# Merging the state weightings of an S4 channel loop on VectorE, and moving a state copy to ScalarE

## The chip, the cores and the metric

The kernel runs on one core of a Trainium2 chip. A core has five engines that run their own instruction streams: TensorE (PE in the profile, its weight loads PEld), VectorE (DVE), ScalarE (ACT), GpSimd (POOL) and SyncE (SP, which issues DMAs here). They wait for each other by semaphores. The metric is the device time of one execution in microseconds, lower is better. The kernel before has a median of 2704.61 us in three runs (2699.75 to 2706.55).

## The reference, cut to what matters

The program computes a gated mix of an attention block and of a state space convolution (S4), and all gradients of it. The part in question is the S4 branch:

```
P = exp(logdA[:, :, None] * l)                 # D channels, N = 128 states, L = 2048 steps
K = einsum("dn,dnl,dn->dl", C, P, dt * B).real # a convolution kernel for each channel
y = irfft(rfft(u) * rfft(K)) + u * Dskip       # causal convolution, D = 576
out = g * attention(x) + (1 - g) * y           # g: a sigmoid gate for each token
```

The kernel computes the convolution and its gradients without a Fourier transform. The 2048 steps are cut into 16 blocks of 128. Inside a block of steps matmuls do the work; from block to block each state is multiplied by z^128 (a complex number per channel and state) and the next block's contribution is added. That is a scan over 15 steps for each channel, run once for the forward direction (called h) and once for the gradient (called g). The scanned states are weighted by w = C * dt * B * z, complex again, and go into matmuls that give y and the gradient of u.

## The kernel before, in words

The program has four stages. The first (up to about 120 us) projects x, prepares the per-channel parameters and stores them in a DRAM tensor `par_d`. The second is attention, forward and backward, to about 2090 us. Beside it GpSimd builds a basis `E_d` for the channel loop. The third, from about 2090 to 2532 us, is the channel loop. The last computes the parameter gradients and the output projections.

The channel loop (L1479) goes over 18 blocks of 32 channels, `i` being the block; states lie on the 128 partitions. Its order on TensorE, ScalarE, VectorE and GpSimd is written out by hand: instructions stand in each engine's queue as the loop emits them. An iteration works on several blocks: it weights and uses the scanned states of block `i`, it scans the second half of block `i` together with the first half of block `i + 1`, and it prepares the input states of block `i + 2` (`sb`) and the loads of block `i + 3` (`mb`).

What the change and the steps of the prediction touch, in the order of an iteration:

- `scan_open` (L707 to L711) makes the tile `HG` of a block's scanned states (real and imaginary part, 15 steps, two directions, 32 channels, float32, two buffers) and copies the first step's states from `UV`, on VectorE. It is called for block `i + 1` at the start of iteration `i`.
- `scan` (L713 to L735) has three VectorE instructions for each step of a chain: a product with the parameter rows 0 to 3 into `tz` (L730), the new input added (L733), and the sum of both parts into `HG` (L735), which reads the second part with its real and imaginary halves reversed. Two chains run alternately, 7 steps each, 42 instructions for an iteration.
- `rw1` (L745 to L750) weights the finished states of block `i` with two real parameter rows. It makes `wa` = `HG` times row 4 and `wb` = `HG` times row 5, 1920 elements each on every partition.
- `rw2` (L752 to L756) makes `Rw`, the complex product in bfloat16, from the halves of `wa` and `wb`: the real half by a subtraction, the imaginary half by -1 and a subtraction, 960 elements each.
- `turn_e` (L658, TensorE transposes and ScalarE copies of the basis into `E1e`), `t0` (L779), `ybp` (L788, matmuls of `Rw` into `yp`), `uv` (L691, matmuls `uvp` and ScalarE evacuations into `UV`, L705).
- `cast1` (L737) casts the states of each direction to bfloat16 (`hR`, `gR`) on ScalarE.
- `pairs1` and `pairs2` (L822 to L840) have VectorE multiply states with states into two tiles `pq`, which lie in the same memory as `wa` and `wb` (tags `wA` and `wB`, one buffer each), and TensorE sums them into `misc`.
- `sums` (L848) has GpSimd add up results of block `i - 1` in two small instructions (L851, L852); `m_part` (L614) and `prep_rx` (L592) feed later blocks, with ScalarE evacuations `mst` and `RX`.
- `load_par` (L673) brings two blocks' parameter rows 0 to 7 from `par_d` into one of two buffers, on GpSimd's DMA queue. Rows 6 and 7 hold weights for another product (`wk_cast`, L758), rows 8 and 9 are read outside the loop.

In the first stage `pars` (L316) fills `par_d` in eleven steps; the last one (L360 to L363) writes rows 4 and 5. In the last stage VectorE, ScalarE and GpSimd are ordered by a scheduler; two row tiles `rowb` and `rowb2` hold outputs 10 and 11 before their stores (L1729 to L1732), and both are used again near the end (L1796).

Of the kernel before, what the change touches and what calls it, by code (L numbers as in the profile page):

```python
# [17 lines left out]
P = 128  # L18


def build(tc, aps, dbg_aps=None, stages=("s1", "attn", "post", "s4", "final")):
# [40 lines left out]
    with ExitStack() as gctx:  # L62
# [27 lines left out]
        NS = NB - 1  # L90
        SUB = 16
        NSUB = P // SUB
        NPAR = 10
        INV2PI = float(1.0 / (2.0 * np.pi))
        MW = P + SUB
        EQ = 4
# [32 lines left out]
        with ExitStack() as ctx:  # L129
# [186 lines left out]
            def pars(k):  # L316
                prm, dt_b, ath, tp, Wn, wz = [prm_t[n_] for n_ in ("prm", "dt", "ath", "tp", "W", "wz")]
                gm, c_, s_, q_ = [zt[:, y] for y in range(4)]
                bc = dt_b.unsqueeze(1).to_broadcast([P, 2, D])
                if k == 0:  # L320
                    AC.activation(dt_b, prm_t["tmpb"], ACT.Exp)
                    tt(ath, prm[:, 0:2, :], bc, A.mult)
                elif k == 1:
                    for y, p_ in enumerate((1, P)):
                        AC.activation(gm[:, y, :], ath[:, 0, :], ACT.Exp, scale=float(p_))
                        V.tensor_scalar(s_[:, y, :], ath[:, 1, :], float(p_) * INV2PI, None, op0=A.mult)
                    V.tensor_scalar(c_, s_, MAGIC, -MAGIC, op0=A.add, op1=A.add)
                elif k == 2:
                    tt(s_, s_, c_, A.subtract)
                    AC.activation(c_, s_, ACT.Sin, scale=0.5 * TWO_PI)  # L330
                elif k == 3:
                    AC.activation(q_, s_, ACT.Sin, scale=0.25 * TWO_PI)
                elif k == 4:
                    tt(Wn[:, 2:4, :], prm[:, 4:6, :], prm[:, 2:4, :], A.mult)
                    tt(tp, prm[:, 4:6, :], prm[:, 3:1:-1, :], A.mult)
                    tt(Wn[:, 0, :], Wn[:, 2, :], Wn[:, 3, :], A.subtract)
                elif k == 5:
                    tt(Wn[:, 1, :], tp[:, 0, :], tp[:, 1, :], A.add)
                    tt(Wn[:, 0:2, :], Wn[:, 0:2, :], bc, A.mult)
                    V.tensor_scalar(Wn[:, 2:4, :], Wn[:, 0:2, :], -1.0, None, op0=A.mult)  # L340
                    GP.dma_start(par_d[:, 6:8, :], Wn[:, 2:4, :])
                    GP.dma_start(dt_d, dt_b)
                    GP.dma_start(prm_d, prm)
                elif k == 6:
                    tt(q_, q_, q_, A.mult)
                    V.scalar_tensor_tensor(s_, q_, -0.5, c_, op0=A.add, op1=A.mult)
                elif k == 7:
                    V.scalar_tensor_tensor(s_, s_, -4.0, gm, op0=A.mult, op1=A.mult)
                    tt(c_, c_, c_, A.mult)
                elif k == 8:  # L350
                    V.scalar_tensor_tensor(c_, c_, -0.5, gm, op0=A.add, op1=A.mult)
                    V.tensor_scalar(c_, c_, -2.0, None, op0=A.mult)
                    V.tensor_scalar(q_[:, 1, :], s_[:, 1, :], -1.0, None, op0=A.mult)
                    GP.dma_start(par_d[:, 8:10, :], zt[:, 1:3, 0, :])
                    GP.dma_start(par_d[:, 1:4, :], zt[:, 1:4, 1, :])
                    GP.dma_start(par_d[:, 0:1, :], zt[:, 1:2, 1, :])
                elif k == 9:
                    tt(wz, Wn[:, 0:2, :], zt[:, 1:3, 0, :], A.mult)
                    tt(tp, Wn[:, 0:2, :], zt[:, 2:0:-1, 0, :], A.mult)
                else:  # L360
                    tt(wz[:, 0, :], wz[:, 0, :], wz[:, 1, :], A.subtract)
                    tt(wz[:, 1, :], tp[:, 0, :], tp[:, 1, :], A.add)
                    GP.dma_start(par_d[:, 4:6, :], wz)  # L363

            steps = [(m, which, pr) for m in (0, 4, 1, 2, 3) for which in (1, 0, 2) for pr in range(2)]
            stgs, sqs = {}, {}
# [121 lines left out]
        def basis_ops(pool, k0, k1):  # L488
# [18 lines left out]

            def load_z(k):
                ez[k] = pool.tile([P, 2, CE], F32, tag="ez", bufs=2, name="ez")
                nc.gpsimd.dma_start(ez[k], par_d[:, 8:10, k * CE:(k + 1) * CE])  # L510

            def emit_power(dst, src, lo, n, sq):

# [157 lines left out]
        pars_ = {}  # L671

        def load_par(b, dma=nc.gpsimd.dma_start):  # L673
            par = pars_[b] = Q["pl"].tile([P, 8, XB], F32, tag="par", bufs=2, name="par")
            dma(par, par_d[:, 0:8, b * XB:(b + 1) * XB])

        def par_of(b):
            return pars_[b // 2][:, :, b % 2 * CB:(b % 2 + 1) * CB]
# [28 lines left out]
        def scan_open(b):  # L707
            B_ = blk(b)
            HG = B_["HG"] = Q["pw"].tile([P, 2, NS, 2, CB], F32, tag="HG", bufs=2, name="HG")
            UVk = B_["UVk"] = B_["UV"][:, :, 0:2 * NB, :].rearrange("p r (s k) c -> p r s k c", s=2)  # L710
            nc.vector.tensor_copy(HG[:, :, 0], UVk[:, :, :, 0, :])  # L711

        def scan(*chains):  # L713

# [29 lines left out]

        def rw1(b):  # L745
            B_ = blk(b)
            for nm, r_, tg in (("wa", 4, "wA"), ("wb", 5, "wB")):
                B_[nm] = Q["pw"].tile([P, 4 * NS, CB], F32, tag=tg, name=nm)
                nc.vector.tensor_tensor(B_[nm], B_["HG"].rearrange("p r k s c -> p (r k s) c"),  # L749
                                        par_of(b)[:, r_, :].unsqueeze(1).to_broadcast([P, 4 * NS, CB]), op=A.mult)  # L750

        def rw2(b):  # L752
            B_ = blk(b)
            wa, wb, Rw = B_.pop("wa"), B_.pop("wb"), B_["Rw"]
            nc.vector.tensor_tensor(Rw[:, 0], wb[:, 2 * NS:], wa[:, 0:2 * NS], op=A.subtract)
            nc.vector.scalar_tensor_tensor(Rw[:, 1], wa[:, 2 * NS:], -1.0, wb[:, 0:2 * NS], op0=A.mult, op1=A.subtract)  # L756

        def wk_cast(b):  # L758
            wk = blk(b)["wk"] = Q["pw"].tile([P, 2, CB], BF, tag="wk", bufs=2, name="wk")
            nc.scalar.copy(wk, par_of(b)[:, 6:8, :])  # L760

        def k0(b):

# [58 lines left out]
        def pairs1(b):  # L822
            B_ = blk(b)
            UV, hR, gR = B_["UV"], B_["hR"], B_["gR"]
            B_["pq"] = pq = [Q["pw"].tile([P, 2, 2, 2, NS, CB], BF, tag=tg, name="pq") for tg in ("wA", "wB")]
            pmul(pq[0][:, 0], UV[:, :, CV0:CV0 + NS, :], hR)
            psum(b, 0, [pq[0][:, 0]], NS)

# [581 lines left out]
        if "s4" in stages:  # L1410
# [8 lines left out]
            with ExitStack() as ctx:  # L1419
# [27 lines left out]
                with tc.manual_schedule(engines={mybir.EngineType.SP}):  # L1447
# [114 lines left out]
        if "final" in stages and "s4" in stages:  # L1562
# [7 lines left out]
            with ExitStack() as ctx:  # L1570
# [33 lines left out]
                with ExitStack() as actx:  # L1604
# [22 lines left out]
                    rowb = tile_("rowb", [P, D], BF, "dlrowb")[0:1]  # L1627
                    rowb2 = tile_("rowb2", [P, D], BF, "ddsrowb")[0:1]
# [3 lines left out]
                    nc.sync.dma_start(zB, par_d[:, 8:10, :])  # L1632
# [7 lines left out]
                    nc.sync.dma_start(Wri, par_d[:, 6:8, :])  # L1640
# [84 lines left out]
                    for u, (f0, fsz) in enumerate(HALF):  # L1725
                        rp = pps.tile([P, 512], F32, tag="one", name="fr")
                        mm(rp[0:1, 0:fsz], lhsT=ones_f[:, 0:1], rhs=Tb[:, f0:f0 + fsz])
                        nc.vector.tensor_tensor(row[:, f0:f0 + fsz], rp[0:1, 0:fsz], dt_b[0:1, f0:f0 + fsz], op=A.mult)
                    nc.vector.tensor_copy(rowb, row)  # L1729
                    nc.gpsimd.dma_start(aps_out["out_10"].rearrange("(o d) -> o d", o=1), rowb)  # L1730
                    nc.vector.tensor_copy(rowb2, dDs_row)
                    nc.gpsimd.dma_start(aps_out["out_11"].rearrange("(o d) -> o d", o=1), rowb2)  # L1732

                ctx.enter_context(tc.manual_schedule(engines={mybir.EngineType.PE}))
                for t in range(NT):
# [57 lines left out]
                    nc.vector.tensor_copy(dgwb[HP * j:HP * j + 1, :], pgw[HP * j:HP * j + 1, 0:DQ])  # L1793
                    nc.sync.dma_start(aps_out["out_12"][j * DQ:(j + 1) * DQ].rearrange("(o d) -> o d", o=1), dgwb[HP * j:HP * j + 1, :])
                for c, (f0, fsz) in enumerate(dch[0:nf]):
                    ob = tile_(("row", "rowb", "rowb2")[c % 3], [P, D], BF, "dwo_bf")  # L1796
# [17 lines left out]
                ob = tile_(("row", "rowb", "rowb2")[c % 3], [P, D], BF, "dwo_bf")  # L1814
# [52 lines left out]
```

## Time and profile before

| what | value |
| --- | --- |
| runs, median (lowest to highest) | 2704.61 us (2699.75 to 2706.55) |
| the profiled execution, its own time | 2687.22 us |
| its span | 2685.5 us, mean granted TensorE clock 0.972 |
| busy: TensorE, VectorE, ScalarE, GpSimd | 2404.0 (90%), 2299.9 (86%), 2345.2 (87%), 1787.2 (67%) us |
| chain that ended last, by engine | ACT 40%, PE 25%, DVE 24% |
| 0 to 167 us (first stage and start of attention) | PE busy 140.45, DVE 90.83, ACT 94.41 |
| 167 to 2050 us (attention) | PE busy 1689.53, DVE 1684.16, ACT 1858.98 |
| 2142 to 2350 us (channel loop) | PE busy 200.24, DVE 199.27, ACT 186.72, POOL 87.93 |
| 2350 to 2530 us (channel loop) | PE busy 169.84, DVE 177.03, ACT 137.76, POOL 79.72 |
| 2530 to 2685.5 us (last stage) | PE busy 145.45, DVE 98.05, ACT 27.07 |
| `wa` and `wb`, 18 each | median 2359 and 2351 ns (2159 and 2151 at least) |
| `Rw`, its two halves | median 1158 and 1151 ns |
| `HG` copy (L711), 18 | median 227 ns |

The profiled execution is one run of its own, shorter than the three timed ones. Every duration below is from it. A row of the order of time gives the start in us, the busy time of the row's instructions in us, the engine, the line, the operation, what it writes and reads with partitions x elements, how many instructions are merged, and in brackets how long the engine was idle before it and what ended that. A row of a stretch of time gives, after the stretch and its length, busy time and count for PE, PEld, DVE, ACT and POOL, then the granted clock, the busy share of the DMA engines and their GB/s. An engine's instructions are issued a little before the one ahead of them has ended, so neighbouring rows overlap by up to 0.2 us.

### The profile page before, as it was taken

How to read it: one execution, taken by the hardware profiler on the slowest of the kernel's cores; microseconds unless marked ns; L12 is line 12 of the kernel's file. 1: busy time of each engine (PE TensorE's matmuls, PEld its weight loads, DVE VectorE, ACT ScalarE, POOL GpSimd, SP SyncE). 2: the span in 40 equal slices, each digit the busy share in tenths (PEclk: the TensorE clock that was granted, in tenths of full speed). 3: DMA queues.
4: the chain of work that ended last, by engine and by line, in shares of the span. 5: the costliest groups of instructions: out<-in, count | busy, mean ns of one | idle time of the engine just before them, and what ended most of it. 6: DMA issues, size and time to landing. Idle time of an engine off the chain costs nothing.

```text
span 2685.5 us, 70035 instructions
## 1 busy us (share of the span) xinstructions
PE 2404.0 (90%) x27411; PEld 1141.2 (42%) x27411; DVE 2299.9 (86%) x4142; ACT 2345.2 (87%) x2727; POOL 1787.2 (67%) x2827
## 2 busy tenths in 40 slices
PE   8798898998988899988999989989887699999999
PEld 4433333333333333333333333333332598998656
DVE  4749999999998999989999988999997599999964
ACT  5489999999999999999999999999995498989221
POOL 0178888888888788888888888887831144444331
PEclk8989999999999999999999999999997699999999
DMA  7637889879979978997898898789669788988995
GB/s 230 189 96 157 155 162 180 165 152 184 172 153 168 181 161 159 177 175 152 167 177 152 161 171 163 155 163 180 149 138 199 182 243 251 254 253 247 268 260 129
DMA packets 1156229, 485.45 MB, mean 181 GB/s; under 512 B 1070517, under 2 KB 1110054, under 8 KB 1153594
## 3 DMA queue, kind: packets, MB, share of 16 engines
q1 hardware_dynamic: 1110138, 341.36, 64.2%
q0 software_dynamic: 43744, 134.11, 18.5%
q10 hardware_dynamic: 2016, 5.51, 0.6%
q8 instruction: 214, 3.51, 0.6%
q14 instruction: 117, 0.96, 0.1%
HBM read 145.68 MB, written 93.21 MB: 89 GB/s over the span
## 4 chain that ended last, share of the span: by engine, by line
ACT 40%; PE 25%; DVE 24%; issue 6%; DMA 3%; SPq 1%; ACTq 0%; POOL 0%; DVEq 0%; POOLq 0%
ACT eb L1384 24%; ACT PT L1379 15%; DVE ds L1389 8%; PE ps_P L30 7%; DVE tz L730 3%; PE accV L30 2%; PE ps_dx L30 2%; PE turn_p L1092 2%; DVE tz L733 2%; DVE HG L735 1%; DVE pq L810 1%; DVE wa L749 1%; PE accK L30 1%; DVE wb L749 1%; DVE dvacc L1146 1%
## 5 line engine op out<-in xcount | busy, mean ns | idle before, releaser
L1389 DVE TENSOR_TENSOR ds<-ps_P,PT 128x512 bf16<-128x512 f32 x2048 | 1312.2, 683 | 120.8 <-PE ps_P L30 83.2
L1384 ACT ACTIVATE eb<-ps_P 128x1024 bf16<-128x1024 f32 x1024 | 1101.4, 1076 | 30.3 <-PE ps_P L30 30.3
L1379 ACT ACTIVATE PT<-ps_P 128x1024 bf16<-128x1024 f32 x1024 | 1106.8, 1081 | 19.4 <-PE ps_P L30 18.0
L30 PE MATMUL ps_P<-dOaT,VaT_g 32*128 32x512 bf16 x2048 | 580.4, 386 | 32.2 <-DVE ds L1389 16.6
L503 POOL TENSOR_TENSOR et<-eG,eT 128x448 f32<-128x448 f32 x576 | 542.2, 961 | 10.7
L30 PE MATMUL ps_P<-QaT_g,KaT_g 32*128 32x512 bf16 x2048 | 401.7, 385 | 138.0 <-ACT PT L1379 124.4
L30 PE MATMUL ps_P<-KaT_g,QaT_g 32*128 32x512 bf16 x2048 | 404.1, 387 | 1.2 <-ACT eb L1384 0.6
L30 PEld LDWEIGHTS <-KaT_g 32*128 32x128 bf16 x2048 | 147.9, 91 | 467.6 <-issue 452.0
L503 POOL TENSOR_TENSOR Eo<-et,et 128x448 bf16<-128x448 f32 x288 | 326.9, 1135 | 20.7
L30 PEld LDWEIGHTS <-QaT_g 32*128 32x128 bf16 x2048 | 116.1, 91 | 283.0 <-issue 260.4
L30 PE MATMUL accV<-eb,dOa 128*32 128x512 bf16 x2048 | 184.9, 394 | 27.4 <-ACT eb L1384 27.3
L30 PE MATMUL accO<-PT,Vtok_g 128*32 128x512 bf16 x2048 | 206.5, 392 | 0.1
L30 PE MATMUL accK<-dsT,Qtok_g 128*32 128x256 bf16 x4096 | 161.5, 278 | 14.1 <-DMA dsT<-ds 12.4
L30 PE MATMUL accQ<-ds,Ktok_g 128*32 128x512 bf16 x2048 | 159.9, 390 | 2.3 <-DVE dvacc L1146 2.2
L30 PEld LDWEIGHTS <-Vtok_g 128*32 128x32 bf16 x2048 | 52.7, 93 | 222.7 <-issue 222.7
L1097 DVE COPY dsT<-turn_p 128x1024 bf16<-128x1024 bf16 (+1 forms) x216 | 139.2, 644 | 2.7 <-PE turn_p L1092 2.7
L1092 PE MATMUL turn_p<-ident_bf,ds 128*128 128x128 bf16 x1664 | 133.7, 223 | 1.9 <-DVE gb L1164 1.0
L669 ACT COPY E1e<-etp 128x1024 bf16<-128x1024 bf16 x132 | 125.1, 1052 | 4.6 <-PE etp L668 4.4
L503 POOL TENSOR_TENSOR et<-eT 128x32 f32<-128x32 f32 (+3 forms) x288 | 115.9, 422 | 11.4
L30 PEld LDWEIGHTS <-Qtok_g 128*32 128x32 bf16 x4096 | 87.5, 96 | 78.6 <-issue 64.9
L1092 PEld LDWEIGHTS <-ds 128*128 128x128 bf16 x1664 | 96.9, 99 | 49.3 <-issue 49.3
L1044 POOL TENSOR_TENSOR dOa<-dO_b,rl 128x288 bf16<-128x288 bf16 x32 | 21.5, 672 | 143.7 <-DVE rl L1039 143.6
(292 smaller groups left out, 3742.0 us busy)
## 6 DMA issues: line engine op xcount, KB each, us to landing
E_d<-Eo POOLq DMA_DIRECT2D x144, 256.0 KB, 3.5
E1n<-E_d POOLq DMA_DIRECT2D x30, 1024.0 KB, 7.4
T0w<-Kp_d SPq DMA_DIRECT2D x18, 1024.0 KB
xs<-xb_d POOLq DMA_DIRECT2D x28, 512.0 KB, 9.9
dsT<-ds SPq DMA_TRANSPOSE x512
dqkv_d<-dtk POOLq DMA_DIRECT2D x96, 72.0 KB, 4.2
Md_d<-mst SPq DMA_DIRECT2D x18, 288.0 KB
skw<-Md_d SPq DMA_DIRECT2D x72, 64.0 KB
```

The source lines that it names most:

```text
L30: return nc.tensor.matmul(out, lhsT=lhsT, rhs=rhs, start=start, stop=stop, **kw)
L503: nc.gpsimd.tensor_tensor(out, a, b, op=op)
L669: copy(E_[:, 4 * q:4 * q + 4], pt_)
L730: nc.vector.tensor_tensor(tz[x], HG[:, :, k - 1].unsqueeze(1).to_broadcast([P, 2, 2, n, CB]), ZZ.unsqueeze(3).to_broadcast([P, 2, 2, n, CB ...
L733: nc.vector.tensor_tensor(tz[x][:, 0], tz[x][:, 0], UVk[:, :, :, k, :], op=A.add)
L735: nc.vector.tensor_tensor(HG[:, :, k], tz[x][:, 0], tz[x][:, 1, ::-1], op=A.add)
L749: nc.vector.tensor_tensor(B_[nm], B_["HG"].rearrange("p r k s c -> p (r k s) c"), par_of(b)[:, r_, :].unsqueeze(1).to_broadcast([P, 4 * NS ...
L1092: nc.tensor.transpose(pt_[:, x, qb, :], t_[:, qb * P:(qb + 1) * P], ident_bf)
L1097: (nc.scalar.copy if NTOT <= now[0] < NTOT + OFF else nc.vector.tensor_copy)(o_(), pt_[:, x:x + n])
L1379: nc.scalar.activation(U["PT"][i, j // 2], ps, ACT.Exp)
L1384: nc.scalar.activation(e, ps, ACT.Exp)
L1389: nc.vector.tensor_tensor(U["ds"][i][:, j, :], ps, U["PT"][i, j // 2][:, j % 2, :], op=A.mult)
```

## The change

The parameter rows get the signs: `par_d` has 12 rows, rows 4 to 7 are -wr, -wr, -wi, wi, and what stood in rows 6 to 9 stands in rows 8 to 11. With these, one VectorE instruction makes both weightings in a tile `wab` (3840 elements on every partition, `HG` read twice, the row of each part read by a broadcast), and one more adds part 0 and the reversed part 1 into both halves of `Rw` (1920 elements). The copy of the first states goes to ScalarE for all blocks but the first, and stands directly behind the evacuation of the states it reads, one iteration earlier than before. The products `pq` and `wab` share one memory of the size of the two before. To make room for the two more parameter rows, the row of output 11 shares `rowb` with that of output 10, output 11 being stored first.

```diff
@@ pars, last step
-                    GP.dma_start(par_d[:, 4:6, :], wz)
+                    V.tensor_scalar(tp, wz, -1.0, None, op0=A.mult)
+                    GP.dma_start(par_d[:, 4:5, :], tp[:, 0:1, :])
+                    GP.dma_start(par_d[:, 5:7, :], tp)
+                    GP.dma_start(par_d[:, 7:8, :], wz[:, 1:2, :])
@@ load_par
-            par = pars_[b] = Q["pl"].tile([P, 8, XB], F32, tag="par", bufs=2, name="par")
-            dma(par, par_d[:, 0:8, b * XB:(b + 1) * XB])
+            par = pars_[b] = Q["pl"].tile([P, 10, XB], F32, tag="par", bufs=2, name="par")
+            dma(par, par_d[:, 0:10, b * XB:(b + 1) * XB])
@@ scan_open
-            nc.vector.tensor_copy(HG[:, :, 0], UVk[:, :, :, 0, :])
+            (nc.vector.tensor_copy if b == 0 else nc.scalar.copy)(HG[:, :, 0], UVk[:, :, :, 0, :])
@@ rw1
-            for nm, r_, tg in (("wa", 4, "wA"), ("wb", 5, "wB")):
-                B_[nm] = Q["pw"].tile([P, 4 * NS, CB], F32, tag=tg, name=nm)
-                nc.vector.tensor_tensor(B_[nm], B_["HG"].rearrange("p r k s c -> p (r k s) c"),
-                                        par_of(b)[:, r_, :].unsqueeze(1).to_broadcast([P, 4 * NS, CB]), op=A.mult)
+            wab = B_["wab"] = Q["pw"].tile([P, 2, 2, 2 * NS, CB], F32, tag="wA", name="wab")
+            h_ = B_["HG"].rearrange("p r k s c -> p r (k s) c").unsqueeze(1).to_broadcast([P, 2, 2, 2 * NS, CB])
+            w_ = par_of(b)[:, 4:8].rearrange("p (m r) c -> p m r c", r=2).unsqueeze(3).to_broadcast([P, 2, 2, 2 * NS, CB])
+            nc.vector.tensor_tensor(wab, h_, w_, op=A.mult)
@@ rw2
-            wa, wb, Rw = B_.pop("wa"), B_.pop("wb"), B_["Rw"]
-            nc.vector.tensor_tensor(Rw[:, 0], wb[:, 2 * NS:], wa[:, 0:2 * NS], op=A.subtract)
-            nc.vector.scalar_tensor_tensor(Rw[:, 1], wa[:, 2 * NS:], -1.0, wb[:, 0:2 * NS], op0=A.mult, op1=A.subtract)
+            wab, Rw = B_.pop("wab"), B_["Rw"]
+            nc.vector.tensor_tensor(Rw, wab[:, 0], wab[:, 1, ::-1], op=A.add)
@@ pairs1
-            B_["pq"] = pq = [Q["pw"].tile([P, 2, 2, 2, NS, CB], BF, tag=tg, name="pq") for tg in ("wA", "wB")]
+            pq = Q["pw"].tile([P, 4, 2, 2, NS, CB], BF, tag="wA", name="pq")
+            B_["pq"] = pq = [pq[:, 0:2], pq[:, 2:4]]
@@ channel loop
                     uv(1, 1)
+                    scan_open(1)
...
                         if nx:
-                            scan_open(i + 1)
                             scan((i, KH, NS, None), (i + 1, 1, KH, None))
...
                         if sb is not None:
                             uv(sb, 1)
+                            scan_open(sb)
@@ last stage
-                    nc.vector.tensor_copy(rowb, row)
-                    nc.gpsimd.dma_start(aps_out["out_10"].rearrange("(o d) -> o d", o=1), rowb)
                     nc.vector.tensor_copy(rowb2, dDs_row)
                     nc.gpsimd.dma_start(aps_out["out_11"].rearrange("(o d) -> o d", o=1), rowb2)
+                    rowb = tile_("rowb", [P, D], BF, "dlrowb")[0:1]
+                    nc.vector.tensor_copy(rowb, row)
+                    nc.gpsimd.dma_start(aps_out["out_10"].rearrange("(o d) -> o d", o=1), rowb)
```

The remaining lines of the diff move the rows 6 to 9 to 8 to 11 where they are written and read, and let the last stage's output tile take the memory of `Tb` where it took that of `rowb2`.

More of the change, by code (lines that the diff above doesn't have):

```diff
@@ L92, in build @@
         NSUB = P // SUB
-        NPAR = 10
+        NPAR = 12
         INV2PI = float(1.0 / (2.0 * np.pi))
@@ L340, in pars @@
                     V.tensor_scalar(Wn[:, 2:4, :], Wn[:, 0:2, :], -1.0, None, op0=A.mult)
-                    GP.dma_start(par_d[:, 6:8, :], Wn[:, 2:4, :])
+                    GP.dma_start(par_d[:, 8:10, :], Wn[:, 2:4, :])
                     GP.dma_start(dt_d, dt_b)
@@ L353, in pars @@
                     V.tensor_scalar(q_[:, 1, :], s_[:, 1, :], -1.0, None, op0=A.mult)
-                    GP.dma_start(par_d[:, 8:10, :], zt[:, 1:3, 0, :])
+                    GP.dma_start(par_d[:, 10:12, :], zt[:, 1:3, 0, :])
                     GP.dma_start(par_d[:, 1:4, :], zt[:, 1:4, 1, :])
@@ L509, in load_z @@
                 ez[k] = pool.tile([P, 2, CE], F32, tag="ez", bufs=2, name="ez")
-                nc.gpsimd.dma_start(ez[k], par_d[:, 8:10, k * CE:(k + 1) * CE])
+                nc.gpsimd.dma_start(ez[k], par_d[:, 10:12, k * CE:(k + 1) * CE])
             def emit_power(dst, src, lo, n, sq):
@@ L746, in rw1 @@
             B_ = blk(b)
-            for nm, r_, tg in (("wa", 4, "wA"), ("wb", 5, "wB")):
-                B_[nm] = Q["pw"].tile([P, 4 * NS, CB], F32, tag=tg, name=nm)
-                nc.vector.tensor_tensor(B_[nm], B_["HG"].rearrange("p r k s c -> p (r k s) c"),
-                                        par_of(b)[:, r_, :].unsqueeze(1).to_broadcast([P, 4 * NS, CB]), op=A.mult)
+            wab = B_["wab"] = Q["pw"].tile([P, 2, 2, 2 * NS, CB], F32, tag="wA", name="wab")
+            h_ = B_["HG"].rearrange("p r k s c -> p r (k s) c").unsqueeze(1).to_broadcast([P, 2, 2, 2 * NS, CB])
+            w_ = par_of(b)[:, 4:8].rearrange("p (m r) c -> p m r c", r=2).unsqueeze(3).to_broadcast([P, 2, 2, 2 * NS, CB])
+            nc.vector.tensor_tensor(wab, h_, w_, op=A.mult)
         def rw2(b):
             B_ = blk(b)
-            wa, wb, Rw = B_.pop("wa"), B_.pop("wb"), B_["Rw"]
-            nc.vector.tensor_tensor(Rw[:, 0], wb[:, 2 * NS:], wa[:, 0:2 * NS], op=A.subtract)
-            nc.vector.scalar_tensor_tensor(Rw[:, 1], wa[:, 2 * NS:], -1.0, wb[:, 0:2 * NS], op0=A.mult, op1=A.subtract)
+            wab, Rw = B_.pop("wab"), B_["Rw"]
+            nc.vector.tensor_tensor(Rw, wab[:, 0], wab[:, 1, ::-1], op=A.add)
         def wk_cast(b):
             wk = blk(b)["wk"] = Q["pw"].tile([P, 2, CB], BF, tag="wk", bufs=2, name="wk")
-            nc.scalar.copy(wk, par_of(b)[:, 6:8, :])
+            nc.scalar.copy(wk, par_of(b)[:, 8:10, :])
         def k0(b):
@@ L1626, in build @@
                     row = tile_("row", [P, D], F32, "dlrow")[0:1]
-                    rowb = tile_("rowb", [P, D], BF, "dlrowb")[0:1]
-                    rowb2 = tile_("rowb2", [P, D], BF, "ddsrowb")[0:1]
+                    rowb2 = tile_("rowb", [P, D], BF, "ddsrowb")[0:1]
                     pfw = Q["pbw"] = ctx.enter_context(tc.tile_pool(name="pfw", reuse_waits="tile", bufs=2))
                     nc.sync.dma_start(zA, par_d[:, 0:4:2, :])
-                    nc.sync.dma_start(zB, par_d[:, 8:10, :])
+                    nc.sync.dma_start(zB, par_d[:, 10:12, :])
                     nc.sync.dma_start(wo_sb[:, 0:nf, :], wo[0:nf * P, :].rearrange("(c p) n -> p c n", p=P))
@@ L1639, in build @@
                     nc.sync.dma_start(O_tok[:, :, 0:D], O_d)
-                    nc.sync.dma_start(Wri, par_d[:, 6:8, :])
+                    nc.sync.dma_start(Wri, par_d[:, 8:10, :])
                     Wr_n, Wi_n = Wri[:, 0, :], Wri[:, 1, :]
@@ L1728, in build @@
                         nc.vector.tensor_tensor(row[:, f0:f0 + fsz], rp[0:1, 0:fsz], dt_b[0:1, f0:f0 + fsz], op=A.mult)
+                    nc.vector.tensor_copy(rowb2, dDs_row)
+                    nc.gpsimd.dma_start(aps_out["out_11"].rearrange("(o d) -> o d", o=1), rowb2)
+                    rowb = tile_("rowb", [P, D], BF, "dlrowb")[0:1]
                     nc.vector.tensor_copy(rowb, row)
                     nc.gpsimd.dma_start(aps_out["out_10"].rearrange("(o d) -> o d", o=1), rowb)
-                    nc.vector.tensor_copy(rowb2, dDs_row)
-                    nc.gpsimd.dma_start(aps_out["out_11"].rearrange("(o d) -> o d", o=1), rowb2)
                 ctx.enter_context(tc.manual_schedule(engines={mybir.EngineType.PE}))
@@ L1795, in build @@
                 for c, (f0, fsz) in enumerate(dch[0:nf]):
-                    ob = tile_(("row", "rowb", "rowb2")[c % 3], [P, D], BF, "dwo_bf")
+                    ob = tile_(("row", "rowb", "Tb")[c % 3], [P, D], BF, "dwo_bf")
                     for u, (e0, esz) in enumerate(HALF):
@@ L1813, in build @@
                            start=(t == 0), stop=(t == NT - 1), tile_position=(0, u * HB))
-                ob = tile_(("row", "rowb", "rowb2")[c % 3], [P, D], BF, "dwo_bf")
+                ob = tile_(("row", "rowb", "Tb")[c % 3], [P, D], BF, "dwo_bf")
                 nc.scalar.copy(ob[0:HB, 0:DH2], ps[0:HB, 0:DH2])
```

## The prediction

> **What bounds the kernel now.** I read the page's top for the share of each engine, then the busy time by stage, then the waits and the order of time of the stage that the change touches.
>
> ```profile
> core 0: us, PE busy (x) PEld busy (x) DVE busy (x) ACT busy (x) POOL busy (x), PEclk, DMA share, GB/s
> 167.00:2050.00 1883.00, 1689.53 (x18160) 589.08 (x18159) 1684.16 (x2780) 1858.98 (x2016) 1527.01 (x2495) 0.99 0.85 163
> 2142.00:2350.00 208.00, 200.24 (x3687) 188.27 (x3680) 199.27 (x472) 186.72 (x292) 87.93 (x84) 0.98 0.85 246
> ```
>
> Attention (167 to 2050 us) is ScalarE's, 99% busy, and the change leaves its order alone. The channel loop (2142 to 2530) is 18 blocks, 13 of which take 21.84 us each from one `wa` to the next; VectorE, TensorE and ScalarE all stand over 90% there. So the question is which link closes the loop from block to block. VectorE in one block, then the TensorE and ScalarE rows that lie beside it:
>
> ```profile
> 2345.98 2.35 DVE L749 TENSOR_TENSOR wa<-HG,par 128x1920 f32<-128x1920 f32 x1
> 2348.25 2.35 DVE L749 TENSOR_TENSOR wb<-HG,par 128x1920 f32<-128x1920 f32 x1
> 2350.64 1.16 DVE L755 TENSOR_TENSOR Rw<-wb,wa 128x960 bf16<-128x960 f32 x1
> 2351.72 1.15 DVE L756 SCALAR_TENSOR_TENSOR Rw<-wa,wb 128x960 bf16<-128x960 f32 x1
> 2352.97 2.23 DVE L810 TENSOR_TENSOR pq<-UV,hR 128x1920 bf16<-128x1920 bf16 x2
> 2355.12 1.15 DVE L810 TENSOR_TENSOR pq<-UV,gR 128x1920 bf16<-128x1920 bf16 x1
> 2356.19 1.16 DVE L838 TENSOR_TENSOR pq<-gR,hR 128x896 bf16<-128x896 bf16 x2
> 2357.33 0.23 DVE L711 CAST HG<-UV 128x128 f32<-128x128 bf16 x1
> 2357.47 0.75 DVE L730 TENSOR_TENSOR tz<-HG,par 128x256 f32<-128x256 f32 x2
> ```
>
> ```profile
> 2351.85 0.21 PE L30 MATMUL yp<-Rw,E1n 128*128 128x30 bf16 x1
> 2352.92 1.82 PE L30 MATMUL yp<-Rw,E1n 128*128 128x30 bf16 x31 [0.86 <-DVE Rw L756]
> 2354.57 1.97 PE L30 MATMUL uvp<-RX,E1e 128*128 128x64 bf16 x32
> ```
>
> ```profile
> 2355.23 2.07 ACT L705 ACTIVATE UV<-uvp 128x512 bf16<-128x512 f32 x4 [0.51 <-PE uvp L30]
> 2357.16 2.02 ACT L599 COPY RX<-RXn 128x1024 bf16<-128x1024 bf16 x1
> ```
>
> `Rw` ends at 2351.72 + 1.15 = 2352.87, 6.89 us after `wa` began. From there two chains run to the next scan. One is TensorE, then ScalarE: `yp`, `uvp`, `UV` ends at 2357.30, which is 4.43 after `Rw`. The other is VectorE's own five products, over at 2357.35. The first-state copy L711 starts at 2357.33, 0.03 after `UV` and about 0.06 after VectorE could have taken it. So VectorE never shows a wait here, and yet both chains arrive together: work taken off VectorE between `Rw` and the scan is worth only what the other chain also loses. Only the stretch from `wa` to `Rw`'s end is on both.
>
> TensorE waited 0.86 us for `Rw` (its row), so it is not the bound until a block is about 0.9 us shorter. In the stretches 2256.5 to 2280.4 and 2389.7 to 2412.7, of 23.9 and 23.0 us, the granted clock is 0.93 instead of 1.00: there TensorE is late.
>
> **The weightings.** Today one block has two 1920-element products and two 960-element sums. Without disturbance (the last block):
>
> ```profile
> 2518.60 2.16 DVE L749 TENSOR_TENSOR wa<-HG,par 128x1920 f32<-128x1920 f32 x1
> 2520.68 2.15 DVE L749 TENSOR_TENSOR wb<-HG,par 128x1920 f32<-128x1920 f32 x1
> 2522.86 1.16 DVE L755 TENSOR_TENSOR Rw<-wb,wa 128x960 bf16<-128x960 f32 x1
> 2523.94 1.15 DVE L756 SCALAR_TENSOR_TENSOR Rw<-wa,wb 128x960 bf16<-128x960 f32 x1
> ```
>
> Durations are 2.00 + 0.16 for 1920 elements and 1.00 + 0.16 for 960: one element per 0.96 GHz cycle and a fixed part. But starts are closer: `wa` to `wb` 2.08, `Rw` to `Rw` 1.08 (fixed part 0.08, since neither needs the other), and `wb` to `Rw` 2.18 (0.18, since it does). All four: 2525.09 - 2518.60 = 6.49. After: 3840 elements, then the dependent sum of 1920: 4.00 + 0.18 + 2.00 + 0.16 = 6.34. Merging drops just the two cheap boundaries, 0.15 per block. The element count is the same, and nothing suggests that the broadcast or reversed patterns are slower: `wa` reads its parameters by a broadcast, and L735 a reversed half, at one element per cycle (293 ns for 128).
>
> [...] Summed as durations, two instructions less are 0.31 per block and the copy 0.23, together 0.54, over 17 blocks 9.2 us. The starts say that about half of a fixed part lies under the neighbour, and I take them: 0.15.
>
> In the middle blocks `wa` and `wb` each take 0.20 more (2.35). GpSimd's two small sums lie beside them:
>
> ```profile
> 2344.61 1.71 POOL L851 TENSOR_TENSOR SS<-m 128x96 f32<-128x96 f32 x1
> 2346.28 2.31 POOL L852 TENSOR_TENSOR SS<-m 128x96 f32<-128x96 f32 x1
> ```
>
> All of the first sum's executions (minimum, median and maximum in ns):
>
> ```profile
> L851 POOL TENSOR_TENSOR SS<-m x17: 404/1762/5967, 2167.7 to 2514.5; 128x96 f32<-128x96 f32 x17
> ```
>
> Undisturbed they take 0.40 (minimum 404 ns). In this block the first ends 0.34 after `wa` starts, the second 0.34 after `wb` starts: each gets in at an instruction's start and delays it 0.20. [...] I keep two delays of 0.20, one at the product, one at the sum: 6.74 against 6.89, still 0.15. If one slips into the products (0.06 to 0.1 of slack) a block gains at most 0.1 more; at 0.40 each it loses 0.40.
>
> TensorE's first `yp` matmul now waits for the whole `Rw`, so 32 instead of 31 follow: 1.82 / 31 = 0.06 later.
>
> **The first states on ScalarE.** VectorE loses 0.23 of work, 0.14 by starts. ScalarE's new copy stands directly behind the last `UV` and needs it. Nearest row: ScalarE's `CK` copy L1510, 128 elements, 0.29 to 0.35. With 0.03 ahead and 0.04 to VectorE: the second `tz` (the only one that waits for it) starts 0.36 after `UV`'s end. Today it starts at about 2357.80, 0.50 after. Gain 0.14 on that chain; bounds for the copy are 0.23 (L776, 32 elements) and 0.47 (L650), so 0.20 to -0.05. Behind the copy stand `RX`, `yd` and the `misc` evacuations, 0.2 later; they end in ScalarE's wait of 1.40 us for `psM` before `mst`, which hides it. Without that cover it would be 0.2 per block.
>
> Per block: second `tz` at 6.74 + 4.43 + 0.06 + 0.36 = 11.59 after the product's start, then 10.02 of scan as now (2357.80 to 2367.82): 21.61 against 21.84, 0.23 less. VectorE's own chain would allow 6.74 + 0.10 + 4.30 + 0.33 + 10.02 = 21.49, so ScalarE's copy closes the loop, not VectorE.
>
> **What costs nothing.** One tile for the products: the merged product now waits for the last reads of all four product tiles; TensorE has ended them some 6.3 us earlier, in the middle of the scan (without this cover, whatever of 6.3 is lost). Parameter loads of 10 instead of 8 rows come over a block ahead; GpSimd waited 2.31 us for `wb` to issue them and will wait about as long. Stage 1 gains a negation, 1152 elements (0.76, L340), and two more GpSimd DMA issues (0.56, L363): VectorE idles 0.66 and 1.56 us soon after, and GpSimd 14 us. In the last stage the row for output 10 waits for the store of output 11, which was issued at 2533.6 and landed 7.5 us later, against 2578.3. All zero; at most 0.8 together.
>
> **Sum.** 13 blocks at 0.23: 3.0. Blocks 0, 5 and 11, where TensorE is late, get the copy's 0.14 each: 0.4. Blocks 16 and 17, with no next state, 0.15 each: 0.3. Together 3.7 us: 2687.2 to 2683.5 in the profiled execution. That one lies 17.4 under the median of the runs, 2704.6, so 2700.9 there.
>
> **Rivals.** [...] 0.18. (b) TensorE's throttle: one more stretch at 0.93 costs 1 to 2 us, as the two do now (23.9 and 23.0 against 21.84), and leaves 2703; less waiting makes TensorE denser. 0.14. (c) Slower: ScalarE's copy is the late link. Nothing lies behind `UV` but it; if the second `tz` came over 0.50 + 0.15 = 0.65 after `UV` the block would lose. At 1.0 (copy at 0.47, waits of 0.25 on either side) that is 0.35 x 15 = 5 us, 2710; 0.3% takes 1.2. Against: L1510's 0.29, and ScalarE's 0.51 of idle just before. 0.10. That the change does not do what it says is excluded by the order of the built program: VectorE has 52 instructions less, ScalarE 17 more.
>
> **The numbers.** The forecast (2 to 6 us less) has 0.58. About 0.3%, 8.1 us, is what a measurement can tell from no change. Faster by more: most of (a), 0.17. Slower by more: the far part of (c) and what I did not see, 0.08. Within: 0.75. The range runs from (a) with a margin, 2694, to (b) with the runs' own spread of some 4 us, 2707.
>
> **What would show it.** `wab` about 4.36 and `Rw` about 2.36 beside GpSimd's sums (4.16 and 2.16 in the last block); `wab` to `Rw`'s end 6.74; block period 21.6; the second `tz` released by ScalarE's `HG`; TensorE's wait for `Rw` down to about 0.6. A period of 21.3 or less, or `wab` above 4.6, would prove me wrong.

## The result, and the profile after

The changed kernel takes 2688.6 us (median of 20 runs, 2678.8 to 2702.3). The kernel before, run beside it and counted with its first three runs, has 2695.2 us in 20 runs (2691.3 to 2706.6; 2694.7 in the 17 without those three). The ratio is 0.9973, with a 95% interval of 0.9962 to 0.9985: 6.6 us less, where 3.7 less was predicted. The predicted 2700.9 lies 12.3 us too high, and the range of 2694 to 2707 does not hold the time. Two steps went wrong, and the larger is not about the change at all. "That one lies 17.4 under the median of the runs, 2704.6, so 2700.9 there" took the median of three runs for the kernel's level, and it lies 9.4 us above the median of 20. The smaller is that the change brought more than the sum allowed.

The profiled execution took 2685.73 us, its span is 2683.9 (before: 2687.22 and 2685.5). The stretch of the loop that was shown of before (its length; busy time and count of PE, PEld, DVE, ACT and POOL; the granted clock; DMA share; GB/s):

```profile
2142.00:2350.00 208.00, 196.64 (x3684) 185.69 (x3685) 199.11 (x459) 188.90 (x300) 104.33 (x84) 0.99 0.87 251
```

VectorE has 13 instructions fewer in it and is as busy as before (199.27): the engines' shares do not show the gain, only the length of the blocks does. Next the order of time of VectorE in one block of the channel loop, the one that answers to the block shown of before (start in us, busy us, engine, line, operation, shapes, instructions merged):

```profile
2346.23 4.34 DVE L753 TENSOR_TENSOR wab<-HG,par 128x3840 f32<-128x3840 f32 x1
2350.61 2.23 DVE L758 TENSOR_TENSOR Rw<-wab 128x1920 bf16<-128x1920 f32 x1
2352.94 2.23 DVE L812 TENSOR_TENSOR pq<-UV,hR 128x1920 bf16<-128x1920 bf16 x2
2355.09 1.15 DVE L812 TENSOR_TENSOR pq<-UV,gR 128x1920 bf16<-128x1920 bf16 x1
2356.16 1.16 DVE L841 TENSOR_TENSOR pq<-gR,hR 128x896 bf16<-128x896 bf16 x2
2357.22 0.87 DVE L733 TENSOR_TENSOR tz<-HG,par 128x256 f32<-128x256 f32 x2
```

`Rw` ends at 2350.61 + 2.23 = 2352.84, 6.61 us after the product began (6.89 before, 6.74 predicted). The five pair products follow as they did. The two `tz` are new in kind: together they span 0.87 instead of 0.75, because the second waits. For what, ScalarE's order of time in the same block shows:

```profile
2355.24 2.06 ACT L708 ACTIVATE UV<-uvp 128x512 bf16<-128x512 f32 x4 [0.43 <-PE uvp L30]
2357.34 0.30 ACT L714 CAST HG<-UV 128x128 f32<-128x128 bf16 x1
```

`UV` ends at 2357.30, the copy runs from 2357.34 to 2357.64, and the second `tz` starts 0.36 after the end of `UV`, as predicted (0.50 before). The block lasts 21.47 us. Ten of the blocks 1 to 15 last 21.46 to 21.52, where before most lasted 21.84 and the prediction had 21.61. TensorE in the same block:

```profile
2352.89 1.87 PE L30 MATMUL yp<-Rw,E1n 128*128 128x30 bf16 x32 [0.87 <-DVE Rw L758]
```

All 32 `yp` matmuls now stand behind the whole `Rw` (31 before). The wait for `Rw` was 0.34 to 0.93 in most blocks, about 0.7 in the middle. And the two groups of the merged instructions over all 18 blocks (minimum, median and maximum in ns):

```profile
L753 DVE TENSOR_TENSOR wab<-HG,par x18: 4153/4345/4359, 2145.8 to 2516.0; 128x3840 f32<-128x3840 f32 x18
L758 DVE TENSOR_TENSOR Rw<-wab x18: 2157/2230/2237, 2150.0 to 2520.2; 128x1920 bf16<-128x1920 f32 x18
```

The minima are blocks without GpSimd's sums beside them. GpSimd's second sum in the same form:

```profile
L855 POOL TENSOR_TENSOR SS<-m x17: 392/4296/4306, 2173.2 to 2513.7; 128x96 f32<-128x96 f32 x17
```

It now waits out the whole product and takes 4.30 us (2.31 before). Beside the sums the product is 0.19 longer, as predicted, but the merged sum only 0.07 and not 0.20. That is the first sign of where the additional gain comes from.

Over the loop, from the first product's start to the last one's, 370.24 us against 376.41: 6.2 less. Of this the undisturbed blocks explain about 5.4: 13 blocks by 0.36, blocks 0, 5 and 11 by the copy's 0.14 (the prediction's figure, which a block that TensorE holds up cannot show) and block 16 by 0.27. Block 17's 0.15 lies behind the last product's start and brings the sum to 5.5. The rest lies in the blocks where TensorE is late, which are not the same ones from run to run (the last experiment).

### The profile page after: what moved, and what is told of

Its sections match the earlier page's. It is cut to its first block, busy times and chain, and to the rows that moved or that the text cites. A ratio compares the mean times of both kernels' runs of the same rounds, so it can differ in the third digit from the quotient of the medians.

```text
span 2683.9 us, 69949 instructions
## 1 busy us (share of the span) xinstructions
PE 2404.7 (90%) x27411; PEld 1137.9 (42%) x27411; DVE 2293.8 (85%) x4090; ACT 2350.8 (88%) x2744; POOL 1818.0 (68%) x2829
## 4 chain that ended last, share of the span: by engine, by line
ACT 40%; PE 28%; DVE 18%; issue 6%; DMA 4%; POOL 2%; SPq 1%; ACTq 0%; DVEq 0%; POOLq 0%
ACT eb L1387 23%; ACT PT L1382 14%; DVE ds L1392 7%; PE ps_P L30 7%; PE accV L30 2%; PE ps_dx L30 2%; PE turn_p L1095 2%; PE ps_dwq L30 2%; DVE tz L733 2%; PE ps_proj L30 2%; DVE wab L753 2%; PE yp L30 2%; PE accK L30 1%; DVE dvacc L1149 1%; DVE tz L736 1%
## 5 line engine op out<-in xcount | busy, mean ns | idle before, releaser
L30 PE MATMUL accK<-dsT,Qtok_g 128*32 128x256 bf16 x4096 | 162.3, 279 | 14.5 <-DMA dsT<-ds 12.4
L1047 POOL TENSOR_TENSOR dOa<-dO_b,rl 128x288 bf16<-128x288 bf16 x32 | 21.5, 673 | 149.9 <-DVE rl L1042 149.9
```

The source lines that it names most:

```text
L30: return nc.tensor.matmul(out, lhsT=lhsT, rhs=rhs, start=start, stop=stop, **kw)
```

## The experiments

The periods of the blocks separate the theories, not the times of single executions: those of one kernel spread over more than 20 us (2678.8 to 2702.3 above), while an undisturbed block's period repeats within 0.06 us. Where no number of runs is given, a kernel ran once (2681 to 2699 us, the late copy apart).

**Each half of the change alone.** First the merging without the move; the copy stays on VectorE, ahead of the scan:

```
-            (nc.vector.tensor_copy if b == 0 else nc.scalar.copy)(HG[:, :, 0], UVk[:, :, :, 0, :])
+            nc.vector.tensor_copy(HG[:, :, 0], UVk[:, :, :, 0, :])
...
                         if nx:
+                            scan_open(i + 1)
...
                             uv(sb, 1)
-                            scan_open(sb)
```

> The merged weightings alone, the first-state copy on VectorE at its old place. Theory (the loop closes from the sum's end over yp, uvp, UV and then the copy): the sum ends 6.61 us after the product's start, UV at 11.08, the copy starts 0.03 later, the second tz at 11.59, and a block takes 21.61. That is 0.13 more than with the copy on ScalarE (21.48) and 0.23 less than before (21.84). Rival (the merging was worth the 0.15 that I predicted, and the copy's move the rest): 21.69.

Measured: `Rw` ends at 6.61, `UV` at 11.08, period 21.61 to 21.65 in the undisturbed blocks. VectorE's order of time at the end of a block of this kernel whose product started at 2349.11:

```profile
2359.05 1.15 DVE L841 TENSOR_TENSOR pq<-gR,hR 128x896 bf16<-128x896 bf16 x2
2360.24 0.23 DVE L714 CAST HG<-UV 128x128 f32<-128x128 bf16 x1
2360.39 0.75 DVE L733 TENSOR_TENSOR tz<-HG,par 128x256 f32<-128x256 f32 x2
```

The copy starts 0.04 after the pair products' end, and as long after `UV`'s. So even with 0.28 less between the product and `Rw`, VectorE and `UV` still arrive together. The merging alone is worth 0.22 per block (21.84 to 21.62): 0.28 at `Rw`, of which 0.05 is given back up to `UV`, because all `yp` matmuls now stand behind the whole `Rw`.

Then the move without the merging; the weightings and their sums are those of before:

```
-            nc.vector.tensor_copy(HG[:, :, 0], UVk[:, :, :, 0, :])
+            (nc.vector.tensor_copy if b == 0 else nc.scalar.copy)(HG[:, :, 0], UVk[:, :, :, 0, :])
...
                         if nx:
-                            scan_open(i + 1)
...
                             uv(sb, 1)
+                            scan_open(sb)
```

> The first-state copy on ScalarE alone, the weightings as before. Theory: Rw ends at 6.89 as before, UV at 11.32, the second tz 0.36 later at 11.68, a block takes 21.70, 0.14 less than before. Rival (VectorE's own work sets the pace): 21.64, since its own chain would let the second tz start at 11.62.

Measured: `Rw` ends at 6.89 as before, the period is 21.69 to 21.72 in the undisturbed blocks, 0.13 under before. ScalarE and then VectorE of this kernel in the block that starts at 2342.53:

```profile
2351.77 2.06 ACT L705 ACTIVATE UV<-uvp 128x512 bf16<-128x512 f32 x4 [0.46 <-PE uvp L30]
2353.87 0.30 ACT L711 CAST HG<-UV 128x128 f32<-128x128 bf16 x1
```

```profile
2353.81 0.82 DVE L730 TENSOR_TENSOR tz<-HG,par 128x256 f32<-128x256 f32 x2
```

The copy ends at 2354.17, and the second `tz` starts at 2354.20, 0.36 after `UV`, which ends at 2353.84 (0.51 before). So the 0.14 for the copy was right. The two halves give 0.22 + 0.13 = 0.35, and the whole change gives 0.36: they add up, and neither hides the other.

**Which merging brings it.** The product merged, the sum in two halves of 960 elements:

```
-            nc.vector.tensor_tensor(Rw, wab[:, 0], wab[:, 1, ::-1], op=A.add)
+            for ri in range(2):
+                nc.vector.tensor_tensor(Rw[:, ri], wab[:, 0, ri], wab[:, 1, 1 - ri], op=A.add)
```

> One product for both weightings, but the sum in two halves of 960; the copy on ScalarE. Theory (GpSimd's second small sum costs 0.20 at an instruction that waits for nothing and 0.07 at one that waits for the instruction ahead anyway): it meets the first half of the sum, which waits for the product, so 4.38 + 0.07 + 1.01 + 1.15 = 6.61 to 6.68, a block 21.48 to 21.55. Rival (each small sum costs 0.20 wherever it meets VectorE): 6.81, a block 21.68.

Measured: `Rw` ends at 6.67 to 6.69, the period is 21.49 to 21.53 in all blocks from 1 to 14. The group of the half sums:

```profile
L759 DVE TENSOR_TENSOR Rw<-wab x36: 1140/1154/1239, 2147.5 to 2517.7; 128x960 bf16<-128x960 f32 x36
```

The first half, which needs the product ahead of it, is the one with up to 1239 ns, 0.07 to 0.08 more than undisturbed; the second stays at 1.15. GpSimd's second sum ends 0.2 after that half starts.

The product in two instructions, the sum merged:

```
-            nc.vector.tensor_tensor(wab, h_, w_, op=A.mult)
+            for m in range(2):
+                nc.vector.tensor_tensor(wab[:, m], h_[:, m], w_[:, m], op=A.mult)
```

> Two products of 1920 as before, but one sum of 1920 for both halves; the copy on ScalarE. Theory: the second small sum meets the second product, which waits for nothing, and costs 0.20 as before: 2.28 + 2.38 + 2.16 = 6.82, a block 21.69. Rival (it is the merged sum that makes the second delay small): 6.69 or less, a block 21.56 or less.

Measured: `Rw` ends at 6.81, the period is 21.68 to 21.70 in the undisturbed blocks. The groups:

```profile
L754 DVE TENSOR_TENSOR wab<-HG,par x36: 2151/2347/2358, 2156.4 to 2530.9; 128x1920 f32<-128x1920 f32 x36
L759 DVE TENSOR_TENSOR Rw<-wab x18: 2157/2158/2159, 2160.7 to 2533.1; 128x1920 bf16<-128x1920 f32 x18
```

Both products have the 0.20 again, and the merged sum has nothing. So GpSimd's second sum gets in at the next of these long VectorE instructions. If that is the second product, which needs nothing from the first, it costs 0.20; if it is the sum, which has to wait for the product anyway, it costs 0.07. Merging the product is worth 0.21 at `Rw`'s end (6.89 to 6.68): 0.08 for the boundary and 0.13 because the second delay moved to a cheaper place. Merging the sum is worth 0.07 to 0.08 there, and most of that is lost again: with half sums only the second half's `yp` matmuls wait, and the period differs by 0.02.

Products and sums are different operations, so the kind of instruction could be the cause instead. That does not fit: in the scan ahead of the last block GpSimd's two sums meet short additions, which need nothing from the one ahead of them either. In the kernel before, the first row has two additions that are hit and the second two that are not:

```profile
2514.61 0.78 DVE L733 TENSOR_TENSOR tz<-tz,UV 128x64 f32<-128x64 f32 x2
2515.31 0.35 DVE L735 TENSOR_TENSOR HG<-tz 128x64 f32<-128x64 f32 x2
```

That is 0.21 for each. A third size came in single blocks: in block 2 of the merging alone, and of the scan from `UV` below, the first sum got in behind the scan's last instruction, the next product started only when that sum ended, and the block was 0.37 and 0.33 longer.

**The same two kernels without GpSimd's sums.** The sums of blocks 0 to 16 into `SS` (part of the parameters' gradients) are left out, first in the changed kernel, then in the kernel before:

```
+            nc.gpsimd.memset(SS, 0.0)
...
-                            sums(i - 1)
+                            m4s.pop(i - 1)
```

> The changed kernel without GpSimd's two small sums in blocks 0 to 16 (their results stay zero, so the parameter gradients built from them are left out). Theory: product 4.16, sum 2.16, the sum ends at 6.34, a block takes 21.21, 0.27 less than with them; over the loop about 4.5 us less. Rival (the longer products have another cause, such as DMA traffic or ScalarE reading the same states): product 4.35 and 21.48 as they are.

> The kernel before without the same small sums (same work left out). Theory: both products 2.16, Rw ends at 6.49, a block takes 21.44, 0.40 less than with them, so that without GpSimd the whole change would be worth 21.44 - 21.21 = 0.23 for a block, which is what I predicted with it. Rival: 2.36 and 21.84 as they are.

Measured: 21.19 to 21.25 after and 21.43 to 21.46 before, in the undisturbed blocks. The changed kernel's groups without the sums:

```profile
L753 DVE TENSOR_TENSOR wab<-HG,par x18: 4140/4157/4167, 2149.2 to 2516.2; 128x3840 f32<-128x3840 f32 x18
L758 DVE TENSOR_TENSOR Rw<-wab x18: 2157/2158/2160, 2153.4 to 2520.4; 128x1920 bf16<-128x1920 f32 x18
```

The sums cost 0.26 per block after and 0.40 before. Without them the whole change is worth 21.44 - 21.22 = 0.22 per block, what the prediction had (0.23) with the sums in place. The 0.14 between this and the measured 0.36 is the cheaper second delay. The loop did not get all of it: from first to last product it took 367.01 us, 3.2 less than the changed kernel's, where 17 blocks by 0.26 would be 4.4. In blocks 1, 4, 5, 10 and 15, of 21.6 to 22.5 us, `UV` came 0.35 to 1.3 late.

**Is ScalarE's copy the closing link?** The copy set behind ScalarE's `RX` copy instead of ahead of it:

```
-                            scan_open(sb)
+                            if mb is None:
+                                scan_open(sb)
...
-                            prep_rx(mb)
+                            prep_rx(mb, mid=lambda: scan_open(sb))
```

> The changed kernel with the first-state copy one ScalarE instruction later, behind the RX copy (1.89 us from start to start). Theory (the copy closes the loop): the second tz moves by 1.89 to 13.34 and a block takes 23.4. Rival (VectorE has the work to fill it, the copy has slack): 21.5 to 21.8.

Measured: 2735.5 us. The second `tz` starts at 13.2 to 14.5 instead of 11.45, and the period is 23.18 at its shortest (blocks 4 and 7) and about 23.9 in most. In blocks 4 and 7 the second `tz` is 1.7 later (1.89 expected) and the block 1.7 longer: the full delay reaches the period. In the others `UV` itself ends up to 1.3 later, and the trace has the reason: each of blocks 1 to 14 except these two has a stretch of 3.4 us with a granted clock of 0.50 (in block 12 from 2459.08 to 2462.49), while blocks 4 and 7 have 1.00 throughout.

The opposite: the scan's first step reads `UV` itself, as two products of 128 elements, and nothing in the scan waits for the copy:

```
+                    if k == 1 and n == 2:
+                        for s in range(2):
+                            nc.vector.tensor_tensor(tz[x][:, :, :, s], UVk[:, :, s, 0, :].unsqueeze(1).to_broadcast([P, 2, 2, CB]),
+                                                    ZZ, op=A.mult)
+                        continue
```

> The changed kernel, but the scan's first step of the next block reads its states from UV itself, as two products of 128 elements in place of one of 256; ScalarE's copy of the first states stays and is needed only by the weightings, a block later. Theory (ScalarE's copy is the link that closes the loop): the first of the two products starts where VectorE is ready, 0.20 after the other chain's (11.20 after the product's start, as in the block without a next state), the second about 0.22 later, the sums 0.08 later than with one instruction: scan 10.03 + 0.08 from 11.20, period about 21.31 in the blocks where TensorE is in time, against 21.48: 0.17 x 13 = 2 us, some 2686.5 where the changed kernel has 2688.6. Rival (TensorE takes over as soon as the copy is out of the way, as when the yp matmuls were split): its wait for Rw goes to nothing, UV comes later than 11.1 in most blocks, and the period stays at 21.45 or above; no time gained.

Measured: 2689.2 us in 12 runs, the kernel before beside it 2693.6; ratio 0.9983 (0.9968 to 0.9997). The period is 21.42 to 21.44 in most blocks: 0.05 less than the changed kernel, not 0.17. VectorE's order of time in the block that starts at 2344.89:

```profile
2355.88 0.41 DVE L738 TENSOR_TENSOR tz<-HG,par 128x256 f32<-128x256 f32 x1
2356.21 0.48 DVE L735 TENSOR_TENSOR tz<-UV,par 128x128 f32<-128x128 bf16 x2
```

The first of the two starts at 2356.21, 0.33 after the `tz` ahead of it, which is as long as that one occupies VectorE; nothing is waited for. I had taken 0.20 from the last blocks, where that `tz` has 128 elements and not 256. So the copy does close the loop, by 0.11 (11.44 against 11.33): with it out of the way VectorE's own chain is next, at 11.33 + 10.03 = 21.36, and the split costs 0.07 of what is gained. The rival is out too: TensorE did not take over, and only blocks 2 to 5 were over 21.5 (in block 2 the scan is 0.33 longer, as said above; in the others `UV` is late).

**Can TensorE give `UV` earlier?** The second group of `uvp` matmuls set after 8 instead of 16 of the first `yp` channels:

```
-                        ybp(i, 0)
-                        if mb is not None:
-                            load_en(mb, 0)
+                        ybp(i, 0, 0, 8)
                         if sb is not None:
                             uv(sb, 1)
                             scan_open(sb)
+                        ybp(i, 0, 8, GS)
+                        if mb is not None:
+                            load_en(mb, 0)
```

> The changed kernel with uv's second half (uvp) behind 8 instead of 16 channels of yp on TensorE, so that UV ends earlier and the copy with it. Theory: UV ends at about 10.75 instead of 11.08, held by ScalarE's E1e copies, then VectorE's own chain closes the loop, second tz at 11.33, a block takes 21.36; in time some 1.5 us (0.06%) less than the changed kernel. Rival (TensorE, which has only about 0.5 us of waiting left in a block, gets a new wait for E1e and becomes the bound): 21.5 or more, and no gain.

Measured: slower than the kernel before, 2704.6 us in 9 runs, ratio 1.0038 (1.0021 to 1.0056). Only block 15 has the 21.36 of the theory; the others have 21.65 to 24.75. TensorE's order of time in one of the worst, whose product started at 2394.69, so that `Rw` was there at 2401.31:

```profile
2400.80 1.56 PE L30 MATMUL yp<-RX,T0w 128*128 128x32 bf16 x22 [1.48 <-issue]
2402.17 3.48 PE L671 MATMUL etp<-ident_bf,E1n 128*128 128x128 bf16 x32
2405.49 1.01 PE L30 MATMUL yp<-Rw,E1n 128*128 128x30 bf16 x16
```

TensorE comes to `Rw` 4.2 late, still busy with what stood ahead in its queue. Part of this is the clock: the 32 `etp` matmuls take 3.48 where they take 1.95 in the next block, in a stretch with a granted clock of 0.50:

```profile
2401.98:2405.39 3.41, 3.41 (x38) 3.41 (x37) 3.41 (x5) 2.14 (x3) 0.00 (x0) 0.50 0.48 109
```

The two other blocks above 23.2 (23.61 and 24.68) have such a stretch as well. The other long blocks have none, and there the rival holds: TensorE is the bound. Over the loop it waits for `E1e` ahead of its `uvp` matmuls ten times, 0.5 each, where the changed kernel has no such wait, and its waits for the load of `E1n` are 6.8 us over the loop (0.4 in the changed kernel). That splitting `yp` frees this tile later, so that its next load is later, is the likely reason for the second; it was not tried alone. My theory for this kernel looked at the chain behind `Rw` only, and is wrong.

**The changed kernel again**, unaltered, beside the kernel before:

> The changed kernel once more, unaltered, beside the kernel before on one chip. Theory (the clean blocks repeat, the late ones are TensorE's and differ from run to run): at least ten blocks between 21.46 and 21.52; those that are longer are others than 1, 5, 8, 10 and 15 in part, and each shows UV, and not VectorE, late; time 0.2 to 0.35% under the kernel before, which again lies nearer 2695 than 2704.6. Rival (the longer blocks belong to the change): the same blocks 1, 5, 8, 10 and 15 are again longer, by the same amounts.

Measured: 2690.8 us in 12 runs against 2693.6 in 23; ratio 0.9989 (0.9974 to 1.0004). Eleven of the blocks 1 to 15 are again at 21.47 to 21.51. The long ones are 3, 5, 8 and 15 (23.02, 21.85, 21.71, 22.60), where the first trace had 1, 5, 8, 10 and 15. So 1, 3 and 10 come and go, and 5, 8 and 15 return: neither expectation is right for all of them. Block 8 is not TensorE: in both traces VectorE's pair products start 0.35 late there. The profile puts the wait down to a copy of `E1e` on ScalarE, which the products do not read, so its cause stays open. Block 3 has a granted clock of 0.93 over its 23.0 us. Block 15 has a row that names its cause. By stretch of time (the length; busy time and count of PE, PEld, DVE, ACT and POOL; the granted clock; DMA share and GB/s):

```profile
2479.50:2487.80 8.30, 5.77 (x103) 5.65 (x101) 8.16 (x5) 7.60 (x11) 4.59 (x2) 1.00 0.64 229
2487.80:2491.00 3.20, 3.20 (x40) 3.20 (x37) 3.11 (x5) 1.79 (x3) 0.00 (x0) 0.58 0.02 8
```

The granted clock falls to 0.58 just while the `uvp` matmuls run, which take 3.22 us instead of 1.97, and `UV` ends at 12.21. Block 15 was also long with the merging alone (22.74), with either merging (22.65 and 22.80) and without the sums, after and before (22.53 and 22.29); it was not in the kernel before, with the copy alone, with the scan from `UV` (21.43) or with `yp` split. Whether the change makes this stretch likelier stays open.

## Why the prediction was wrong, point by point

- **What bounds the loop: right.** The chain from `Rw` over `yp`, `uvp` and `UV` to the second `tz` sets the period. Both halves of the change alone, the late copy and the scan from `UV` agree. VectorE's own chain behind `Rw` has 0.11 to spare in the changed kernel: where its pair products came 0.35 late (block 8), the block was 0.23 longer. Taking work off VectorE there was not tried.
- **"I keep two delays of 0.20, one at the product, one at the sum": this step failed.** The merged sum is delayed 0.07, not 0.20. `Rw` ends at 6.61, not 6.74, and a block takes 21.48, not 21.61: 0.36 less instead of 0.23. The prediction had the neighbour to see it by: it read that a dependent start costs 0.10 more than an independent one, and did not ask whether a delay could lie inside that wait. The kernels above put it there: 0.20 at the second product, 0.07 at the sum, whole or half. It named the case that "one slips" as worth at most 0.1 more; 0.13 came, in every block.
- **The price of merging itself: right.** 0.15 for the two boundaries. With GpSimd's sums out of both kernels `Rw` ends at 6.49 and 6.35, 0.14 apart. Summed as durations the difference is 0.30 (2.16 + 2.15 + 1.16 + 1.15 in the undisturbed block of before, 4.16 + 2.16 of the changed kernel without the sums); half of it lay under the neighbours, as the starts had said. An element costs what it did: 1920 more take 2.00 us more (4157 against 2158 ns). The 9 us of rival (a), from which the lower end of the range was set, are shown by no run: a block is 0.36 shorter, and the two comparisons have 6.6 and 2.8 us less.
- **GpSimd's sums beside the products: unlike for the two engines.** GpSimd's second sum took 4.30 us behind the merged product of 4.34 (2.31 before, behind one of 2.35), and 0.39 undisturbed. VectorE lost less: a sum of 0.40 cost it 0.20 or 0.07, depending on what it would have waited for anyway. Only where a product started at the end of a sum, 0.33 late, did it pay nearly the whole sum.
- **The copy on ScalarE: right**, 0.298 us for 0.29 assumed, and 0.36 from `UV` to the second `tz`. ScalarE's wait ahead of `mst`, which was to hide what stands behind the copy, is still there (1.61 us). Rival (c) is out. "ScalarE's copy closes the loop, not VectorE" holds by 0.11.
- **What was set at nothing: right in the loop, open ahead of it.** No wait of VectorE for TensorE's last reads of the shared tile or for the parameter loads appears in the loop; its waits for `hR` and `gR` are 1.3 and 0.8 us in all (1.1 and 0.8 before). Ahead of the loop, from the start of attention's last `PT` on ScalarE to the first product, the three traces with the old parameter rows (before, the copy alone, before without the sums) take 140.9 to 141.0 us, and the nine with the new ones 141.7 to 147.1. The granted clock falls earlier in the nine: over the 30 us behind that start it is 0.92 to 1.00 in the three and 0.59 to 0.83 in the nine. The rows are of before and of after:

```profile
2001.20:2031.20 30.00, 23.23 (x250) 7.55 (x245) 26.76 (x46) 20.93 (x23) 4.54 (x9) 0.92 0.68 132
2002.40:2032.40 30.00, 25.38 (x231) 7.90 (x230) 24.32 (x41) 19.18 (x21) 1.36 (x2) 0.71 0.60 122
```

No run changes the parameter rows alone, and these are single executions, so whether the change costs 1 to 6 us there stays open.

- **"TensorE's wait for `Rw` down to about 0.6"**: 0.7 in the middle.
- **The sum: short by a third.** 13 blocks at 0.36, not 0.23, and block 16 at 0.27, not 0.15: 5.5 us where the text has 3.7. The measured 6.6 (4.0 to 10.2 by its interval) and 2.8 (-1.1 to 7.0) of the two comparisons, weighted by the widths of their intervals, give a ratio of 0.9979, 5.7 us with some 2.5 either way. That holds 5.5 and 3.7 alike: the larger size rests on the blocks' periods, not on the times. In the first profiled execution 1.5 us show (2687.22 to 2685.73) where the loop alone is 6.2 shorter; what lies ahead of the first product was 3.6 longer in it, and what lies behind the last one's start 0.9.
- **The reference: the largest error.** Of the 17.4 us that the prediction put between the profiled execution and the median, 9.4 belong to the three runs: the median of 20 is 8.0 above it. The three are among the four longest of the 20, and runs of the same kernel beside the experiments have medians of 2693.0 (14) and 2693.6 (23). Why the first three were longer is not on record. The text knew that the profiled execution lay under all three runs shown, and took the three for the level. Against 2695.2 the same sum gives 2691.5, 2.9 above the measured time.
- **Rival (b), the throttle**: stretches of 3.4 us with a granted clock of 0.50 did come in the loop, before (blocks 5 and 11) and after (block 15). Above the undisturbed period the long blocks hold about 3.3 us of the loop before, and 2.6 and 3.3 in the two traces after; no difference can be told.

## What to carry to other kernels

Cost a delay by where it falls: here an instruction that had to wait for its predecessor hid most of it (0.07), one that would have started at once paid 0.20, so look at what a contender will hit once instructions are merged. When two chains arrive at the same point within 0.1 us, price each edit by the chain that it leaves behind, and check the second-latest link before promising more: here VectorE stood 0.11 us behind the copy. A prediction of a few microseconds needs a reference as good: three runs with a spread of 7 us do not give a level to 4.

## What had not been expected of the hardware

GpSimd's two-input sum of 96 elements takes 0.40 us undisturbed and cost VectorE 0.20 us at an instruction that needs nothing from the one ahead of it, and 0.07 us at one that does; twice a product waited for its end, and the block was 0.37 and 0.33 us longer. It waited out a VectorE product of 4.34 us in full and took 4.30 us itself.

Undisturbed blocks repeat within 0.06 us (21.83 to 21.87 before, 21.46 to 21.52 after), and yet executions of one kernel differ by more than 20 us (2678.8 to 2702.3 after). In the kernel before single blocks of the loop grow by up to 2.1 us (block 5, 23.94 against 21.84). Blocks 5 and 11 before, which grew by more than 1 us, hold a stretch of 3.4 us with the granted clock at 0.50, block 3 of the changed kernel again has 0.93 over its 23.0 us and block 15 0.58 over 3.2 us, and in the kernel with the late copy twelve of the blocks 1 to 14 have such a stretch. A gain of 0.26 us per block, as without the sums, is therefore plain in one block's order of time and lost in the time of one execution.
